# Stacking the left-over rows two groups earlier in a spectral filter kernel, with three more trips through memory

## The chip, the cores and the metric

The kernel runs on one core of a Trainium2 chip. The metric is the time of one execution in device microseconds; the time given for a kernel is the median of its runs.

## The reference

```python
h  = x + irfft2(rfft2(layernorm(x)) * (w_r + 1j * w_i))     # x: 2048 x 640, w: 2048 x 321
g, u = layernorm(h) @ w_gate, layernorm(h) @ w_up           # 640 x 1728 each
out = h + (g * u) @ w_down                                  # 1728 x 640
```

All of it is float32. The change lies in the first line, in the part that transforms along the 640 features.

## The kernel before, in words

The two-dimensional transform is done with matrix products. A first stage transforms along the 2048 rows in steps of 128 points. It leaves, for 16 groups `g`, the values of the 640 features folded by symmetry: four blocks of 128 features (`s1`, one for each kind of symmetry) and 128 left-over features, 31 to 33 of each kind (`rest`).

The **feature stage** then goes over the 16 groups. It is a software pipeline whose order is written out by hand: each engine runs its instructions in the order of the code, and a loop turn `g` holds work of four groups.

- `d_mm(g + 2)`, on TensorE (PE): the transform along the features into two banks `re` and `im`. The four main blocks are four float32 products of 160 to 193 columns each (`tab,s`).
- The left-over features are computed in a cheaper single-pass format, `fp32r`. For accuracy each value is split into a high and a low part: `rest_high` (ACT) and `rest_low` (DVE) write `s1r[:, 0]` and `s1r[:, 1]`. The product is then high x high + high x low + low x high.
- In a *plain* group this takes six products over all 128 left-over features and all 322 columns (`frt,s1r`). In a *stacked* group the 33 rows of one kind are laid under each other three times (high, low, high: 99 rows), and each kind needs one product of 160 to 194 columns, four in all (`frt,st`). `ST` holds the stacked groups; `PLAIN` says where they begin.
- To lay rows under each other, data must change partitions, so it goes through DRAM: `spread(a, b)` writes the split rows of groups a to b - 1 to `sfar` (four DMAs, one for each kind), and `stack(g, n, ...)` reads groups g to g + n - 1 back (two DMAs, of 66 and 33 rows). A read is issued only when the writes that it reads have landed.
- `d_out` (ACT) copies `re` and `im` to `t`; `s2_mm(g)` (PE) multiplies by a table (`bits`) into `u`, which from group 1 on has a single buffer; `filt(g)` (DVE, three instructions that read `u`) applies the weights `wts`; `add` (DVE) sums; `is2_mm(g - 1)` (PE, into `ir` and `im`) starts the way back, and `is2_parts` (ACT, DVE, POOL) takes it out to `qr` and `qm`.

The reads are placed by the table `AGAIN`: the key is the loop turn, the value the first group, the number of groups and the place. Before, groups 5 to 7 are read in turn 0 (place `dC`), 8 and 9 in turn 1 (`qt`), 10 to 12 in turn 4 and 13 to 15 in turn 7 (into the two halves of `s1r`, whose first contents are done with by then).

All these DMAs are issued by SyncE (SP), in one order: the tables `bits` (`load_mm`), the weights `wts` (`load_w`), writes and reads. A DMA issue that must wait holds up all that stand behind it. Eight DMAs of this queue can be under way: each waits for the one that was issued eight before it.

Of the kernel before, what the change touches and what calls it, by code (L numbers as in the profile page):

```python
# [12 lines left out]
F32R = mybir.dt.float32r  # L13
# [3 lines left out]
P = 128  # L17
S, D, NF, FF = 2048, 640, 321, 1728
NT = S // P
NG = 16  # L20
# [4 lines left out]
RROWS = ((31, 1), (0, 1), (62, 2), (63, 2))  # L25
RWHERE = ((1, 0), (0, 0), (1, 160), (0, 160))
RW = (160, 194, 162, 162)
PLAIN, MID = 5, 10
IPLAIN, IFAR = 5, 9
SUMS = 7  # L30
IPARTS = ((5, 4), (9, 3), (12, 4))
AGAIN = {0: (5, 3, "dC"), 1: (8, 2, "qt"), 4: (10, 3, 0), 7: (13, 3, 1)}
NR = 4
AHEAD = 5
FOLDS = {0: (1, 2), 1: (3,), 2: (4,), 7: (9,), 9: (11,)}
# [14 lines left out]
def f32(ap):  # L50
    return ap.bitcast(F32)
# [29 lines left out]
def tile_spectral_glu(ctx: ExitStack, tc: tile.TileContext, x, wre, wim, wgu, wlast, wdown, wdlast,  # L81
                      cc, ci, fmain, frem, imain, irem, mm, out):
    nc = tc.nc
# [52 lines left out]
    def home(tag, shape, name, dt=F32):  # L136
        return keep.tile(shape, dt, tag=tag, name=name)

    def cut(t, o, *shape):
        v = t[:, o:o + int(np.prod(shape))]  # L140
        names = [f"d{i}" for i in range(len(shape))]
        return v.rearrange(f"p ({' '.join(names)}) -> p {' '.join(names)}", **dict(zip(names[1:], shape[1:])))
# [6 lines left out]
    s1r = home("wA", [P, 2, NG, P], "s1r", F32R)  # L149
# [142 lines left out]
    def s1_rest(t):  # L292
        act(at(rest, t), PS1[t][1][:, 0:P].rearrange("p (g m) -> p g m", g=32), AF.Copy)
# [5 lines left out]
    def rest_high(a, b):  # L299
        act(s1r[:, 0, a:b], rest[:, a:b], AF.Copy)  # L300

    def rest_low(a, b):
        tt(s1r[:, 1, a:b], rest[:, a:b], f32(s1r[:, 0, a:b]), op=OP.subtract)
# [33 lines left out]
    for t in range(NT):  # L337
# [52 lines left out]
        else:  # L390
            b2a, b2, b3a, a2, b3, a3, m, v = stats[0]
# [6 lines left out]
        s1_mm(t)  # L398
    s1_main(NT - 1, PS1[NT - 1][0], 2, 4)
    s1_rest(NT - 1)  # L400
    for a, b in ((0, 2), (2, PLAIN), (PLAIN, MID)):
        rest_high(a, b)
        rest_low(a, b)

# [2 lines left out]
    def load_w(g):  # L407
        w, j = wts[:, g % 3], g // 2 if g < NG - 2 else g - 7
        i = wts[:, 5 if j == 8 else 3 + j % 2]
        nc.sync.dma_start(w, wre[g])  # L410
        if g % 2 == 0 or g >= NG - 2:
            nc.sync.dma_start(i, wim[j])
        W2[g] = w, i

    def load_mm(g, way):
        if g < NG:
            nc.sync.dma_start(mms[g % 4][:, way], mm[g][:, way])
# [10 lines left out]
    def d_mm(g):  # L428
        ps = PD[g] = bank("re"), bank("im")
        where = ((1, 0), (0, 0), (1, 160), (0, 160))  # L430
        main = [(b, o, FW[c], s1[:, c, g], fmt[:, FOFF[c]:FOFF[c] + FW[c]]) for c, (b, o) in enumerate(where)]
        if g not in ST:
            parts(ps, main, [(b, s1r[:, k, g], frt[:, l, b]) for k, l in ((0, 0), (0, 1), (1, 0)) for b in range(2)])
            return
        parts(ps, main, [])
        for q, ((b, o), w) in enumerate(zip(RWHERE, RW)):
            a = 4 * NQ + sum(RW[:q])
            mmx(ps[b][:, o:o + w], ST[g][0:99, q], frall[0:99, a:a + w], False, q >= 2)

    ST = {}  # L440
    sfar = far.tile([4, 2, 33, NG - PLAIN, P], F32, name="sfar")

    def spread(a, b):
        for q, (r, s) in enumerate(RROWS):
            nc.sync.dma_start(sfar[q, :, :, a - PLAIN:b - PLAIN].rearrange("l r g n -> r l g n"),
                              f32(s1r[r:r + 32 * s + 1:s, :, a:b]))

    def stack(g, n, tag):
        if tag in (0, 1):
            o = s1r[:, tag, NG - 12:NG].rearrange("p (q n) m -> p q n m", q=4)  # L450
        else:
            o = home(tag, [P, 4, n, P], "st", F32R)
        src = sfar[:, :, :, g - PLAIN:g - PLAIN + n].rearrange("q l r g n -> q (l r) (g n)")
        for a, b, r in ((0, 66, 0), (66, 99, 0)):
            nc.sync.dma_start(f32(o[a:b].rearrange("p q g n -> p q (g n)")),
                              src[:, r:r + b - a].rearrange("q r n -> r q n"))
        for i in range(n):
            ST[g + i] = o[:, :, i]

    def d_out(g, parts=(0, 1)):  # L460
        for i in parts:
            if i == 0:
                T[g] = wk([P, 2, NQ], "t")
            for h in range(2):
                act(T[g][64 * i:64 * i + 64, h], PD[g][i][64 * h:64 * h + 64, 0:NQ], AF.Copy)

    def s2_mm(g):
        if g >= NG - 2:
            ps = PU[g] = bank("re"), bank("im")
        elif g == 0:  # L470
            ps = PU[g] = bank("im2", 1), bank("ir2", 1)
        else:
            PU[g] = pools["y"].tile([P, 2, 512], F32, tag="u", name="u", bufs=1)
            ps = PU[g][:, 0], PU[g][:, 1]
        for h in range(2):
            nc.tensor.matmul(ps[h][:, 0:NQ], mms[g % 4][:, 0, h], T[g][:, h], start=True, stop=True)  # L476
# [18 lines left out]
    def filt_half(g, h, alone=False, mid=()):  # L495
        if h == 0:
            Y[g] = wk([P, 2, NQ], "y"), wk([P, 2, NQ], "us")
        y, us = (a[:, h] for a in Y[g])
        v, w, im = PU[g][h][:, 0:NQ], *W2[g]
        direct = lambda: tt(y, v, w[:, h], op=OP.mult)  # L500
        join = lambda: tt(y, y, us, op=OP.add)
        if alone:
            direct()
            for f in mid:
                f()
            nc.vector.scalar_tensor_tensor(us[0:64], v[64:128], -1.0, im[64:128, h], op0=OP.mult, op1=OP.mult)
            tt(us[64:128], v[0:64], im[0:64, h], op=OP.mult)
            return direct, join
        act(us[0:64], v[64:128], AF.Copy, scale=-1.0)
        act(us[64:128], v[0:64], AF.Copy)  # L510
        nc.gpsimd.tensor_tensor(us, us, im[:, h], op=OP.mult)
        return direct, join
# [52 lines left out]
    def is2_out(g):  # L565
        high, end, low, main, edges = is2_parts(g)
        high(copy)
        end(copy)
        low()
        main(slice(0, 4))  # L570
        edges(nc.gpsimd)

    for g in range(4):
        for way in range(2):
            load_mm(g, way)
        if g < 3:
            load_w(g)
    spread(PLAIN, MID)
    d_mm(0)
    d_out(0)  # L580
    d_mm(1)
# [1 line left out]
    for g in range(NG - 1):  # L583
        s2_mm(g)
        load_mm(g + 4, 0)
        if g + 2 < NG:
            d_mm(g + 2)
        if g + 3 == NG:
            xt = home("big", [P, 2, 5, 2, 512], "xt", F32R)
            flat = xt[:, 1].rearrange("p k l n -> p (k l n)")  # L590
            irt, sirt = cut(flat, 0, 5, NQ), cut(flat, 5 * NQ, 4, 162)
            scrap, near = cut(flat, 2258, D), cut(flat, 2258 + D, 4, 4, P)
        if g == NG - 2:
            nc.gpsimd.dma_start(flat[:, 0:2258], irem)
        if g == NG - 2:
            s2_mm(g + 1)
            filt_half(g, 0, True, (lambda: is2_out(g - 2),))
        if g >= 1:
            is2_mm(g - 1)
            load_mm(g + 3, 1)  # L600
        if g < NG - 2:
            add = filt(g)
        else:
            direct, _ = filt_half(g, 1)
            direct()
            late = [filt_half(g + 1, 0), filt_half(g + 1, 1, True)]
            high, end, low, main, edges = is2_parts(g - 1)
            late[0][0]()
            high(copy)
            end(copy)  # L610
            late[0][1]()
            late[1][1]()
            low()
            main(slice(0, 4))
            edges(nc.gpsimd)
        if g + 3 < NG:
            load_w(g + 3)
        if g >= 4 and g in AGAIN:
            stack(*AGAIN[g])
        if g == 0:  # L620
            rest_high(MID, NG)
        elif g == 1:
            rest_low(MID, NG)
            qr = home("qr", [P, 2, NT, P], "qr", F32R)
        if g + 2 < NG:
            d_out(g + 2, (0,))
            if 1 <= g < NG - 3:
                high, end, low, main, edges = is2_parts(g - 1)
                high(copy)
                end(copy)  # L630
            d_out(g + 2, (1,))
            add()
            if 1 <= g < NG - 3:
                low()
                main(slice(0, 4))
                edges(nc.gpsimd)
        if g < 2:
            stack(*AGAIN[g])
        elif g == 2:
            spread(MID, NG)  # L640
        if g == 9:
            nc.sync.dma_start(cit, ci)
            nc.sync.dma_start(imt, imain)
# [252 lines left out]
    for ts in (range(3), range(3, 6), range(6, 8)):  # L896
        n, t0 = len(ts), ts[-1] + 1
# [664 lines left out]
```

## Time and profile before

| | |
|---|---|
| median of 3 runs | 671.57 us (671.43 to 671.62) |
| profiled execution | 671.61 us, of which the profiled span is 669.8 us |
| busy: PE, DVE, POOL, ACT | 99%, 70%, 59%, 48% of the span |
| feature stage, `d_mm(0)` to the last `is2_mm` | 38.3 us to 106.0 us |

Times within the profile count from the start of the span. Busy times of PE overlap, since matrix products are pipelined, so a stretch of PE is measured here from the start of one instruction to the start of another. "SPq" rows are DMA issues: their duration is that of the issue, not of the transfer. In rows of stretches the columns are: stretch, length, busy time (and instructions) of PE, of its weight loads PEld, of DVE, ACT and POOL, then the granted TensorE clock, the mean busy share of the 16 DMA engines, and GB/s.

### The profile page before, as it was taken

Reading aid. Unit: us, or ns where it says so; the run is one execution under the profiler, and the core shown is the slowest. Engines: PE = TensorE matmul, PEld = TensorE weight load, DVE = VectorE, ACT = ScalarE, POOL = GpSimd, SP = SyncE. Lnnn points to the kernel's source line nnn. Section 1 sums busy time; section 2 is a strip of 40 time slices with the busy share of each in tenths; the row PEclk is TensorE's granted clock in tenths of the full one; section 3 lists DMA queues with packets and bytes.
Section 4 is the critical chain, followed back from the end, with each engine's and each line's share of the span. In section 5 each row is a group of like instructions: output and inputs, shape, how many; then the busy total and the mean of one; then the engine's idle time right before and its main releaser. Section 6 shows DMA issues by size and latency. Waiting matters only on the chain.

```text
span 669.8 us, 10242 instructions
## 1 busy us (share of the span) xinstructions
PE 660.0 (99%) x3695; PEld 587.1 (88%) x3695; DVE 468.7 (70%) x951; ACT 321.6 (48%) x621; POOL 394.5 (59%) x379
## 2 busy tenths in 40 slices
PE   6999999999999999999999999999999999999997
PEld 6999999887888888888888899888888888888887
DVE  6969997788767767594857567754757475757644
ACT  6977773585525243453626146634434251624220
POOL 3101124750397977969686445198786869697610
PEclk9999999999999999999999999999999999999999
DMA  8639885502212120042332467212011121212004
GB/s 320 226 109 282 237 252 160 160 1 79 79 40 80 39 79 28 34 99 59 99 78 84 93 134 260 78 41 74 13 37 76 41 78 40 79 40 80 1 0 158
DMA packets 48953, 66.12 MB, mean 99 GB/s; under 512 B 24082, under 2 KB 30670, under 8 KB 48774
## 3 DMA queue, kind: packets, MB, share of 16 engines
q1 hardware_dynamic: 48246, 62.91, 30.5%
q0 software_dynamic: 288, 2.16, 0.8%
q8 instruction: 29, 0.48, 0.3%
q10 hardware_dynamic: 368, 0.39, 0.2%
q14 instruction: 22, 0.18, 0.1%
HBM read 54.61 MB, written 10.84 MB: 98 GB/s over the span
## 4 chain that ended last, share of the span: by engine, by line
PE 95%; ACT 2%; DVE 1%; DMA 1%; issue 0%; POOL 0%; DVEq 0%
PE e L121 50%; PE d L121 26%; PE eo L121 4%; PE y L121 2%; PE re L121 2%; PE u L476 2%; PE im L527 2%; PE im L121 2%; PE im L270 2%; PE ir L527 1%; DMA x<-in_x_dram 1%; ACT s L296 1%; ACT fold L212 0%; ACT fold L211 0%; PE y L803 0%; PE u L527 0%
## 5 line engine op out<-in xcount | busy, mean ns | idle before, releaser
L121 PE MATMUL e<-xt,wst 128*128 128x512 f32 x864 | 211.1, 390 | 0.0
L121 PEld LDWEIGHTS e<-xt,wst 128*128 128x128 f32 x864 | 160.6, 188 | 31.7
L1082 DVE TENSOR_TENSOR x<-d,x 128x320 f32<-128x320 f32 x280 | 120.5, 483 | 41.2 <-PE d L121 37.0
L121 PE MATMUL d<-wd,ht 128*128 128x320 f32 x832 | 142.2, 309 | 0.0
L121 PEld LDWEIGHTS d<-wd,ht 128*128 128x128 f32 x832 | 129.6, 188 | 5.2
L996 POOL TENSOR_TENSOR wst<-raw,wst 128x1024 fp32r<-128x1024 f32 x23 | 55.5, 2412 | 69.5 <-ACT wst L995 69.5
L121 PE MATMUL e<-t,wst 128*128 128x512 f32 x360 | 94.0, 391 | 0.0
L121 PEld LDWEIGHTS e<-t,wst 128*128 128x128 f32 x360 | 66.7, 188 | 13.0
L121 PE MATMUL d<-wt,ht 128*128 128x320 f32 x360 | 69.0, 309 | 0.0
L1012 POOL TENSOR_TENSOR wst<-raw,wst 128x896 fp32r<-128x896 f32 (+1 forms) x46 | 65.3, 1444 | 0.2 <-ACT wst L1007 0.2
L121 PEld LDWEIGHTS d<-wt,ht 128*128 128x128 f32 x360 | 57.3, 188 | 0.8
L1098 ACT ACTIVATE ht<-e 128x512 fp32r<-128x512 f32 x44 | 26.4, 599 | 49.2 <-DVE e L1160 23.7
L1007 ACT ACTIVATE wst<-raw 128x896 fp32r<-128x896 f32 (+1 forms) x48 | 30.1, 676 | 31.2 <-POOL raw L1001 30.5
L1156 DVE TENSOR_TENSOR e<-e,h 128x512 f32<-128x512 f32 x24 | 16.8, 699 | 39.3 <-ACT wst L1007 23.1
L1057 DVE TENSOR_TENSOR x<-d,x 128x320 f32<-128x320 f32 x62 | 27.5, 485 | 22.4 <-PE d L121 22.3
L688 ACT ACTIVATE wd<-draw 128x320 fp32r<-128x320 f32 (+1 forms) x30 | 15.7, 560 | 55.1 <-POOL draw L698 52.4
L121 PE MATMUL e<-xt,wdir 128*128 128x512 f32 x180 | 42.1, 392 | 0.0
L1136 ACT ACTIVATE h<-e 128x512 f32<-128x512 f32 x24 | 14.3, 596 | 56.8 <-PE e L121 56.8
L121 PEld LDWEIGHTS e<-xt,wdir 128*128 128x128 f32 x180 | 33.4, 188 | 7.7 <-ACT xt L813 0.5
L1101 DVE TENSOR_TENSOR ht<-e,ht 128x512 fp32r<-128x512 f32 x54 | 37.0, 686 | 1.6 <-ACT ht L1098 1.3
L1153 ACT ACTIVATE h<-e 128x512 f32<-128x512 f32 x24 | 14.3, 598 | 46.7 <-PE e L121 46.7
L667 POOL TENSOR_TENSOR wd<-draw,wd 128x640 fp32r<-128x640 f32 x8 | 12.4, 1576 | 40.8 <-ACT wd L666 40.8
(239 smaller groups left out, 1188.1 us busy)
## 6 DMA issues: line engine op xcount, KB each, us to landing
raw<-in_wgu_dram SPq DMA_DIRECT2D x24, 640.0 KB
draw<-in_wdown_dram SPq DMA_DIRECT2D x24, 320.0 KB
wts<-in_wre_dram SPq DMA_DIRECT2D x16, 322.0 KB
x<-in_x_dram SPq DMA_DIRECT2D x15, 320.5 KB
out_dram<-x SPq DMA_DIRECT2D x15, 320.0 KB
bits<-in_mm_dram SPq DMA_DIRECT2D x32, 128.0 KB
wts<-in_wim_dram SPq DMA_DIRECT2D x9, 322.0 KB
zfar<-zr SPq DMA_DIRECT2D x32, 80.0 KB
```

The lines of the kernel that those rows point to most:

```text
L121: nc.tensor.matmul(o, l, r, start=start, stop=stop, skip_group_check=True)
L527: nc.tensor.matmul(out, y[:, h, a:b], inv(g, h), start=n == 0, stop=n == len(ys) - 1)
L688: act(o[:, 0, a:a + n], src, AF.Copy)
L996: ptt(wa[:, 1], stage[:, 0:1024], f32(wa[:, 0]), op=OP.subtract)
L1007: act(ws[:, 0, o:o + b - a], stage[:, a:b], AF.Copy)
L1012: ptt(ws[:, 1, o:o + b - a], stage[:, a:b], f32(ws[:, 0, o:o + b - a]), op=OP.subtract)
L1057: tt(xv, ps[b][:, 0:320], xv, op=OP.add)
L1082: tt(xv, o, xv, op=OP.add)
L1098: act(hop[:, a, 0], src, AF.Copy)
L1101: engine.tensor_tensor(hop[:, a, 1], src, f32(hop[:, a, 0]), op=OP.subtract)
L1136: act(h0, oa, AF.Copy)
L1156: tt(ob, ob, h1, op=OP.add)
```

## The change

Groups 3 and 4 become stacked groups (`PLAIN` from 5 to 3). Their rows must be written and read back before the loop begins, so the first write is cut in two: groups 3 to 5 first, then 6 to 9 (`NEXT`). Between the two stand two reads: group 3 alone, and groups 4 and 5 behind it. Both go into the place `dC`, which holds three groups. Groups 6 and 7 are read in turn 1, followed by group 8, which goes to the part of `dC` that group 3 has left; groups 9 to 11 in turn 4, 12 to 14 in turn 6, and 15 in turn 9, into the same part of `dC`. The splits are cut to match, and groups 3 to 5 are split ahead of group 2.

```diff
-PLAIN, MID = 5, 10
+PLAIN, NEXT, MID = 3, 6, 10
...
-AGAIN = {0: (5, 3, "dC"), 1: (8, 2, "qt"), 4: (10, 3, 0), 7: (13, 3, 1)}
+FIRST = ((3, 1, "dC", 0), (4, 2, "dC", 1))
+AGAIN = {1: ((6, 2, "qt", 0), (8, 1, "dC", 0)), 4: ((9, 3, 0, 0),), 6: ((12, 3, 1, 0),), 9: ((15, 1, "dC", 0),)}
...
-    for a, b in ((0, 2), (2, PLAIN), (PLAIN, MID)):
+    for a, b in ((0, 2), (PLAIN, NEXT), (2, PLAIN), (NEXT, MID)):
         rest_high(a, b)
         rest_low(a, b)
...
-    def stack(g, n, tag):
-        if tag in (0, 1):
-            o = s1r[:, tag, NG - 12:NG].rearrange("p (q n) m -> p q n m", q=4)
-        else:
-            o = home(tag, [P, 4, n, P], "st", F32R)
+    SH = {}
+
+    def stack(g, n, tag, at):
+        if tag not in SH:
+            SH[tag] = s1r[:, tag, NG - 12:NG].rearrange("p (q n) m -> p q n m", q=4) if tag in (0, 1) else home(
+                tag, [P, 4, 3 if tag == "dC" else n, P], "st", F32R)
+        o = SH[tag][:, :, at:at + n]
...
-    spread(PLAIN, MID)
+    spread(PLAIN, NEXT)
+    for job in FIRST:
+        stack(*job)
+    spread(NEXT, MID)
     d_mm(0)
```

The other lines of the diff only walk through the new form of the table.

On PE, from `s2_mm(1)` to `s2_mm(2)` (L476 `u<-t`), the products of group 3 read as follows before. `tab,s` are the main products, `frt,s1r` the left-over ones, `ir` and `im` of L527 the way back of group 0.

```order
L121 MATMUL im<-tab,s_89 128x160
L121 MATMUL re<-tab,s_89 128x193
L121 MATMUL im<-tab,s_89 128x161
L121 MATMUL re<-tab,s_89 128x161
L121 MATMUL re<-frt,s1r 128x322
L121 MATMUL im<-frt,s1r 128x322
...
L527 MATMUL ir_647<-bits,y 65x32x4 x2
L527 MATMUL im_646<-bits,y 128x32x4 x4
L476 MATMUL u<-t,bits 128x322 x2
```

Four more left-over products of 322 columns stand in the gap. The same place now (line numbers are one or two higher):

```order
L122 MATMUL im<-tab,s_89 128x160
L122 MATMUL re<-tab,s_89 128x193
L122 MATMUL im<-tab,s_89 128x161
L122 MATMUL re<-tab,s_89 128x161
L122 MATMUL im<-frt,st 128x160
L122 MATMUL re<-frt,st 128x194
L122 MATMUL im<-frt,st 128x162
L122 MATMUL re<-frt,st 128x162
L529 MATMUL ir_653<-bits,y 65x32x4 x2
L529 MATMUL im_652<-bits,y 128x32x4 x4
L478 MATMUL u<-t,bits 128x322 x2
```

Group 3 has four left-over products instead of six, and they read `st`, which a DMA fills; group 4 one turn later likewise.

On SP, from the first write on, the order before is this (`sfar<-s1r` is a write, `st<-sfar` a read of 66 or 33 rows; 128 columns are one group):

```order
L445 DMA sfar<-s1r 33x2x640 x4
L417 DMA bits<-in_mm_dram 128x256
L410 DMA wts<-in_wre_dram 128x644
L455 DMA st<-sfar 66x4x384
L455 DMA st<-sfar 33x4x384
L417 DMA bits<-in_mm_dram 128x256 x2
L410 DMA wts<-in_wre_dram 128x644
L412 DMA wts<-in_wim_dram 128x644
L455 DMA st<-sfar 66x4x256
L455 DMA st<-sfar 33x4x256
```

And now, up to the first load behind the second write:

```order
L446 DMA sfar<-s1r 33x2x384 x4
L458 DMA st<-sfar 66x4x128
L458 DMA st<-sfar 33x4x128
L458 DMA st<-sfar 66x4x256
L458 DMA st<-sfar 33x4x256
L446 DMA sfar<-s1r 33x2x512 x4
L418 DMA bits<-in_mm_dram 128x256
L411 DMA wts<-in_wre_dram 128x644
```

Four reads and four writes have moved ahead of the table of group 4 and the weights of group 3, and the first of these reads stands right behind the write that it reads.

More of the change, by code (lines that the diff above doesn't have):

```diff
@@ L446, in spread @@
                               f32(s1r[r:r + 32 * s + 1:s, :, a:b]))
-    def stack(g, n, tag):
-        if tag in (0, 1):
-            o = s1r[:, tag, NG - 12:NG].rearrange("p (q n) m -> p q n m", q=4)
-        else:
-            o = home(tag, [P, 4, n, P], "st", F32R)
[L453 to L456, printed above, removed]
+    SH = {}
[4 more added lines that the diff above has]
+        o = SH[tag][:, :, at:at + n]
+        src = sfar[:, :, :, g - PLAIN:g - PLAIN + n].rearrange("q l r g n -> (l r) q (g n)")
+        for a, b in ((0, 66), (66, 99)):
+            nc.sync.dma_start(f32(o[a:b].rearrange("p q g n -> p q (g n)")), src[0:b - a])
         for i in range(n):
@@ L617, in tile_spectral_glu @@
             load_w(g + 3)
-        if g >= 4 and g in AGAIN:
-            stack(*AGAIN[g])
+        if g >= 4:
+            for job in AGAIN.get(g, ()):
+                stack(*job)
         if g == 0:
@@ L636, in tile_spectral_glu @@
                 edges(nc.gpsimd)
-        if g < 2:
-            stack(*AGAIN[g])
-        elif g == 2:
+        if g < 4:
+            for job in AGAIN.get(g, ()):
+                stack(*job)
+        if g == 2:
             spread(MID, NG)
```

## The prediction

> **What bounds the kernel now.** I read the page's busy shares and its chain first, then the timeline of PE over the group loop, then DVE and the DMA queue over the same microseconds.
>
> ```profile
> PE 660.0 (99%) x3695; PEld 587.1 (88%) x3695; DVE 468.7 (70%) x951; ACT 321.6 (48%) x621; POOL 394.5 (59%) x379
> PE 95%; ACT 2%; DVE 1%; DMA 1%; issue 0%; POOL 0%; DVEq 0%
> ```
>
> PE is busy for 99% of the span and is 95% of the chain that ended last. What PE is spared in the group loop shortens the run, unless another engine takes the place over at once. So the question is how near the next engine is. The PE timeline from the left-over products of group 3 to those of group 5 (columns: start us, us, what):
>
> ```profile
> 47.70 0.42 PE L121 MATMUL re<-frt,s1r 128*128 128x322 f32 x1
> ...
> 48.70 0.60 PE L527 MATMUL ir<-bits,y 128*65 128x128 f32 x4
> ...
> 50.03 1.25 PE L476 MATMUL u<-t,bits 128*128 128x322 f32 x4
> ...
> 52.16 0.42 PE L121 MATMUL re<-frt,s1r 128*128 128x322 f32 x1
> ...
> 53.16 0.60 PE L527 MATMUL ir<-bits,y 128*65 128x128 f32 x4
> ...
> 54.48 1.25 PE L476 MATMUL u<-t,bits 128*128 128x322 f32 x4
> ...
> 56.61 0.35 PE L121 MATMUL im<-frt,st 99*128 99x160 f32 x1
> ...
> 57.13 0.60 PE L527 MATMUL ir<-bits,y 128*65 128x128 f32 x4
> ...
> 58.47 1.26 PE L476 MATMUL u<-t,bits 128*128 128x322 f32 x4
> ```
>
> Groups 3 and 4 spend 48.70 - 47.70 = 53.16 - 52.16 = 1.00 us on six left-over products of 322 columns. Group 5 is stacked and spends 57.13 - 56.61 = 0.52 us on four. One loop turn is 54.48 - 50.03 = 4.45 us with a plain group and 58.47 - 54.48 = 3.99 us with a stacked one. The same stretch on DVE:
>
> ```profile
> 46.86 0.83 DVE L484 TENSOR_TENSOR y<-u,wts 128x644 f32<-128x644 f32 x1 [0.61 <-PE u L476]
> ...
> 49.42 0.96 DVE L303 TENSOR_TENSOR s1r<-rest,s1r 128x768 fp32r<-128x768 f32 x1
> ...
> 51.61 0.83 DVE L484 TENSOR_TENSOR y<-u,wts 128x644 f32<-128x644 f32 x1
> ...
> 53.32 0.82 DVE L486 TENSOR_TENSOR us<-u,wts 64x644 f32<-64x644 f32 x1
> ...
> 55.77 0.83 DVE L484 TENSOR_TENSOR y<-u,wts 128x644 f32<-128x644 f32 x1 [0.32 <-PE u L476]
> ...
> 57.48 0.82 DVE L486 TENSOR_TENSOR us<-u,wts 64x644 f32<-64x644 f32 x1
> ```
>
> Here the reader sees a second clock. From 46.86 to 51.61 DVE has no gap: the filter of group 1, the split of groups 10 to 15 (0.96 us at 49.42, in this turn alone) and the sums. The filter of group 2 thus begins at 51.61 because DVE is free only then, and it holds `u`, which has one buffer, until 53.32 + 0.82 = 54.14. PE refills `u` at 54.48, only 0.34 us later. In a stacked turn DVE holds it to 57.48 + 0.82 = 58.30, and PE comes at 58.47.
>
> **The change part by part.** *Two groups fewer with six products.* PE is spared 2 x (1.00 - 0.52) = 0.96 us. If all of it counted, the run would take 671.61 - 0.96 = 670.65 us.
>
> *What `u` leaves of it.* Nothing ahead of group 3's products changes on PE, so DVE still starts at 46.86 and still reaches the filter of group 2 at 51.61, and `u` still comes free at 54.14. PE would arrive there at 54.48 - 0.96 = 53.52. It waits, and with some 0.06 us for the hand-over (55.77 against the end of the products at 54.48 + 1.25 = 55.73 shows 0.04) it starts at 54.20. The gain that is left is 54.48 - 54.20 = 0.28 us, and 0.68 us turn into a wait of PE for DVE. One turn later DVE starts at 54.20 + 1.25 + 0.04 = 55.49 and frees `u` at 58.02, while PE comes at 54.20 + 3.99 = 58.19: no second wait, and the 0.28 us stay. This also gives group 3 slack: its products may end 0.68 us later than they could before they cost anything.
>
> *The write and the read that group 3 now needs.* Rows of the DMA queue (SPq, columns as above), of the wait on it, and the two splits on DVE that release the first write:
>
> ```profile
> 39.76 0.56 DVE L303 TENSOR_TENSOR s1r<-rest,s1r 128x384 fp32r<-128x384 f32 x1
> 40.39 0.83 DVE L303 TENSOR_TENSOR s1r<-rest,s1r 128x640 fp32r<-128x640 f32 x1
> 41.25 2.54 SPq L445 DMA_DIRECT2D sfar<-s1r  x4
> 43.89 0.45 SPq L417 DMA_DIRECT2D bits<-in_mm_dram  x1
> 45.26 0.35 SPq L410 DMA_DIRECT2D wts<-in_wre_dram  x1
> 46.63 0.75 SPq L455 DMA_DIRECT2D st<-sfar  x2
> SPq L455 <- DMA sfar<-s1r: 0.9, 1, 0.9
> ```
>
> Stretches of the DMA engines (the last two columns are their busy share and GB/s):
>
> ```profile
> 41.25:42.00 0.75, 0.75 (x7) 0.75 (x6) 0.00 (x0) 0.70 (x3) 0.00 (x0) 1.00 0.00 0
> 42.00:46.00 4.00, 4.00 (x25) 3.59 (x24) 2.70 (x6) 3.23 (x7) 0.00 (x0) 1.00 0.64 196
> 44.00:52.00 8.00, 8.00 (x53) 7.34 (x53) 7.15 (x12) 5.24 (x12) 1.83 (x2) 1.00 0.72 190
> 52.00:72.00 20.00, 20.00 (x142) 18.36 (x141) 18.54 (x26) 15.08 (x37) 3.68 (x10) 1.00 0.95 281
> ...
> 121.00:122.00 1.00, 1.00 (x9) 1.00 (x9) 0.96 (x3) 0.27 (x1) 1.00 (x2) 1.00 0.08 32
> 122.00:125.50 3.50, 3.50 (x23) 3.07 (x22) 3.43 (x9) 2.51 (x5) 3.28 (x3) 1.00 0.68 179
> 125.50:127.00 1.50, 1.50 (x10) 1.29 (x9) 1.12 (x2) 1.50 (x5) 1.46 (x2) 1.00 0.00 0
> 128.50:134.00 5.50, 5.50 (x35) 4.79 (x34) 4.18 (x14) 2.15 (x6) 3.09 (x5) 1.00 0.60 147
> ```
>
> The write of five groups went out at 41.25, when DVE's split of 640 columns had ended (40.39 + 0.83). The new first write needs only the 384 columns in second place, done at 39.76 + 0.56 = 40.32, so it goes out at 40.35. Before, 0.75 us passed with nothing moving, then 4 us of traffic (0.8 us a group), then 0.6 us until the queue was let go at 46.63. Three groups are 0.75 + 2.4 + 0.6 = 3.75 us: done at 44.1. Then group 3 is read. The trace shows a read by itself in the next stage, where three groups of the same shape are issued at the row below and move from 122.0 to 125.5, 1.2 us a group:
>
> ```profile
> 121.06 0.32 SPq L727 DMA_DIRECT2D si<-ifar  x1
> ```
>
> One group is 0.95 + 1.2 + 0.6 = 2.75 us, so its rows are there at 46.85, and PE wants them at 47.70. Bounds: no moving time at all gives 45.65; a moving time set by the number of pieces, which is the same for one group as for three, gives 44.1 + 0.95 + 3.5 + 0.6 = 49.15. I take 46.85, since bytes set it in the two reads that the trace shows alone: three groups are 0.68 x 3.5 = 2.38 us of the engines, four groups in as many pieces (128.5 to 134) are 0.60 x 5.5 = 3.30, a ratio of 1.39 against 1.33 by bytes. With the slack of 0.68 us group 3 may come as late as 48.4.
>
> *Groups 4 and 5 behind it* move 2.4 us more and are there at 46.85 + 2.4 = 49.25. Group 4's products begin at 52.16 - 0.48 = 51.68.
>
> *What is pushed back on the queue.* Eight further issues, the four reads and the second write, now stand ahead of the loads of 43.89 and 45.26. At some 0.4 us each (0.75 for two at 46.63) and 2.54 for the write, the weights of group 3 leave at about 44.1 + 1.6 + 2.5 + 0.5 = 48.7. The DMA engines are behind with older traffic then, so they wait for 3.6 us of reads and 4 x 0.8 = 3.2 us of writes that run from 45.05 to 51.9, and land by some 53.5. Their reader is the filter that started at 55.77, now 55.49. This costs nothing as long as the DMA engines keep up.
>
> *One more piece of the split* (128 + 512 instead of 640 columns) is one more instruction on ACT and on DVE. By the two DVE rows (0.56 us for 384, 0.83 for 640) one costs 0.15 us besides its columns, and DVE idles 0.61 us ahead of 46.86 as cover; ACT's piece is of that size too. *Group 8's read* waits for group 3's products to be done with their place, long past when it is issued. Reads of 9 to 15 move between groups; one of these matters and is the first rival.
>
> Sum: 671.61 - 0.96 + 0.68 = 671.33 us for the profiled execution (span 669.8); against the median of 671.57 that is 671.29. I say 671.3.
>
> **The rivals.** *Group 9 waits for its read: slower.* What was the read of groups 10 to 12 becomes that of 9 to 11, at the same place in the loop and wanted one turn earlier.
>
> ```profile
> 63.49 1.14 SPq L455 DMA_DIRECT2D s1r<-sfar  x2
> ...
> 71.72 0.33 SPq L417 DMA_DIRECT2D bits<-in_mm_dram  x1
> ...
> SPq L417 <- DMA s1r<-sfar: 0.2, 1, 0.2
> ...
> 72.56 0.35 PE L121 MATMUL im<-frt,st 99*128 99x160 f32 x1
> ```
>
> The load at 71.72 had waited for this read, so it took 71.7 - 63.49 = 8.2 us. Group 9's products stand at 72.56, so 72.56 - 63.49 = 9.07 us are there: 0.87 to spare. Ahead of it the DMA engines now have one group more to read (1.2 us) and two more to write (1.6 us), 2.8 in all. From 52 to 72 us they are 95% busy and can't catch up. They can start 0.9 earlier, and the stretch from 44 to 52 is only 72% busy, which holds (0.95 - 0.72) x 8 = 1.8 us. Used fully, 0.1 us is left and the read is in time. If only the early start helps, it is 1.9 late, PE waits 1.9 - 0.87 = 1.0 us, and the run takes 671.33 + 1.0 = 672.35. It decides from 0.87 + 0.28 = 1.15 us of backlog on: then the run is slower than before. Chance 0.26.
>
> The Trainium skill (DMA: Bandwidth & Descriptors, Bandwidth) speaks against the change here: its table has 0.95 us for 64 KB and 6.15 us for 1 MB, so small transfers pay a floor of roughly 0.6 us, an estimate from these two. Two reads more ahead of group 9's would by it add 1.2 us to the 0.1 above, PE would wait 0.4 us, and the run would take some 671.8 us. The rows of before can't separate a floor from the idle 0.95 us ahead of a read, so I leave its weight within this rival.
>
> *Group 3 is late.* If pieces and not bytes set the read, it lands at 49.15, PE idles 49.15 - 47.70 = 1.45 us, 0.48 + 0.48 of it is paid back by shorter products, and `u` is refilled at 54.48 + 1.45 - 0.96 + 0.05 = 55.02: 671.61 + 0.54 = 672.15. Against it speaks the ratio of 1.39 above. Later still, the price grows one for one: a read of 8.2 us, the slowest that a row of before shows (the fence above), would end at 52.3. The Trainium skill (TensorE: Matmul & The Clock Gate, The HAM clock gate) has the clock halved after an idle window of some 3.4 us, which only such a wait of 4.6 us would reach. The stretches above show the granted clock at 1.00 throughout. Chance 0.09.
>
> *The full saving.* If PE did not meet the held `u`, 670.65. The gapless DVE rows from 46.86 to 54.14 speak against it. Chance 0.06.
>
> *Nothing gained*: DVE's chain starts later than the timeline says (its 46.86 start follows PE's `u` of group 1, and ACT and DVE have one more split ahead), by the 0.28 us that are left. 671.6, chance 0.07.
>
> **How the numbers follow.** The forecast keeps 0.52. The range reaches down to 670.9, short of the full saving, and up to 672.9, over most of the late reads; outside lie the full saving (0.06), a third of the group 9 cases and a third of the late group 3 (0.12 together): 0.18. A change under 0.2%, 1.34 us, is about what a measurement of this kernel can't tell from none; no case is faster by that much, 0.02 for what I don't see. Slower by it needs over 672.9, 0.12. The rest, 0.86, is the same. The forecast's own range is 671.0 to 671.6.
>
> **What would show it.** Right: groups 3 and 4 with four left-over products of 0.52 us; a wait of PE of 0.5 to 0.7 us at its `u` refill near 54.2 that is put down to DVE; the first write at 40.35, group 3's read issued near 44.1 and no wait of PE at its products; the end of the group loop about 0.3 us earlier. Wrong: PE waiting for a DMA at the products of group 3 or group 9, DVE waiting for weights, or the loop's end later than before while the stages behind it are unchanged.

## The result and the profile after

The changed kernel takes 676.49 us in the median of seven runs (673.17 to 677.63), beside 671.62 us for the kernel before on the same chip: a ratio of 1.0061 with a 95% interval of 1.0051 to 1.0071. It is slower by some 5 us where 671.3 was forecast. Its runs scatter over 4.5 us; the profiled execution is one of its shorter ones, with 673.93 us and a span of 672.2.

The busy shares and the chain:

```profile
PE 661.6 (98%) x3691; PEld 587.5 (87%) x3691; DVE 468.7 (70%) x952; ACT 321.3 (48%) x622; POOL 394.0 (59%) x379
PE 88%; DMA 4%; ACT 3%; DVE 2%; POOL 1%; issue 1%; SPq 0%; DVEq 0%; ACTq 0%
```

DMAs have grown from 1% to 4% of the chain. The waits of PE in the feature stage that are new (columns: us in total, times, longest):

```profile
PE im L122 <- DMA s1r<-sfar: 1.3, 1, 1.3
PE u L478 <- DVE us L488: 0.4, 1, 0.4
```

The PE timeline shows where:

```profile
47.71 0.35 PE L122 MATMUL im<-frt,st 99*128 99x160 f32 x1
48.23 0.60 PE L529 MATMUL ir<-bits,y 128*65 128x128 f32 x4
...
54.29 1.32 PE L478 MATMUL u<-t,bits 128*128 128x322 f32 x4 [0.42 <-DVE us L488]
...
58.34 1.26 PE L478 MATMUL u<-t,bits 128*128 128x322 f32 x4
...
74.04 0.31 PE L122 MATMUL im<-frt,s1r 99*128 99x160 f32 x1 [1.33 <-DMA s1r<-sfar]
```

Group 3's left-over products start at 47.71 with no wait and take 48.23 - 47.71 = 0.52 us. PE waits for DVE at `u` (54.29). At 58.34 it is 0.13 us ahead of the kernel before. At 74.04 it has waited 1.33 us for the read of groups 9 to 11, and is 74.04 - 72.56 = 1.48 us behind. The stage ends 1.4 us later (107.4 against 106.0). The other 0.9 us of the longer span lie in later stages that the change doesn't touch; I don't explain them. In the profiled executions of the other kernels below these stages take at most 0.7 us longer than before, and where a kernel loses more than 1 us, most of it lies in the feature stage.

SP's queue, in the changed kernel:

```profile
40.36 2.54 SPq L446 DMA_DIRECT2D sfar<-s1r  x4
44.75 1.60 SPq L458 DMA_DIRECT2D st<-sfar  x4
46.39 2.44 SPq L446 DMA_DIRECT2D sfar<-s1r  x4
48.93 0.46 SPq L418 DMA_DIRECT2D bits<-in_mm_dram  x1
...
57.30 3.71 SPq L446 DMA_DIRECT2D sfar<-s1r  x4
...
64.89 0.82 SPq L458 DMA_DIRECT2D s1r<-sfar  x2
...
73.92 0.76 SPq L458 DMA_DIRECT2D s1r<-sfar  x2
```

the row of the third write (groups 10 to 15) in the kernel before:

```profile
55.60 2.65 SPq L445 DMA_DIRECT2D sfar<-s1r  x4
```

and the waits of SP in the changed kernel that bear on it:

```profile
SPq L458 <- DMA sfar<-s1r: 1.7, 1, 1.7
SPq L446 <- DMA wts<-in_wim_dram: 1.0, 1, 1.0
SPq L446 <- DMA st<-sfar: 1.4, 2, 0.8
SPq L458 <- DMA s1r<-sfar: 1.0, 1, 1.0
```

The third write goes out 1.7 us later and its four issues take 1.1 us longer. The first of them waits 1.0 us for the weights that were issued eight places ahead of it, the next two 1.4 us for the read of groups 6 and 7. The read of groups 9 to 11 stands behind this write on SP and needs it landed. It is issued at 64.89, 1.40 us later than the read at the same place before. The profile names no wait of SP between the write and this issue, so as far as the rows show it is the queue's order that makes the read late, and not a wait for the landing. SP's next read waited for this one, so it took until 73.9: 9.0 us from its issue, where it was 8.2. The stretches of the DMA engines (last two columns: busy share and GB/s):

```profile
44.00:48.00 4.00, 4.00 (x26) 3.67 (x26) 3.27 (x7) 2.88 (x6) 1.55 (x1) 1.00 0.32 65
44.00:52.00 8.00, 8.00 (x53) 7.26 (x53) 7.15 (x12) 5.23 (x12) 1.83 (x2) 1.00 0.56 165
```

From 44 to 52 us they carry less than before (0.56 against 0.72), although more was to be moved: SP waits 1.7 us for the first write to land ahead of the read at 44.75, and the table of group 4 and the weights of group 3 leave only from 48.93 on.

### The profile page after: what moved, and what is told of

Same layout as the page of the kernel before. It is cut to its first block, busy times and chain, and to the rows that moved or that the text cites. A ratio compares the mean times of both kernels' runs of the same rounds, so it can differ in the third digit from the quotient of the medians.

```text
span 672.2 us, 10254 instructions
## 1 busy us (share of the span) xinstructions
PE 661.6 (98%) x3691; PEld 587.5 (87%) x3691; DVE 468.7 (70%) x952; ACT 321.3 (48%) x622; POOL 394.0 (59%) x379
## 4 chain that ended last, share of the span: by engine, by line
PE 88%; DMA 4%; ACT 3%; DVE 2%; POOL 1%; issue 1%; SPq 0%; DVEq 0%; ACTq 0%
PE e L122 48%; PE d L122 24%; PE eo L122 4%; PE y L122 2%; PE u L478 2%; PE re L122 2%; PE im L529 2%; PE im L271 2%; PE im L122 1%; DMA s1r<-sfar 1%; DMA z<-zfar 1%; DMA raw<-in_wgu_dram 1%; PE ir L529 1%; DMA x<-in_x_dram 1%; ACT s L297 1%
```

## The experiments

**Is the wait for group 9 the whole loss?** The changed kernel once more:

> The changed kernel once more, to see how its executions spread. In the profile of it PE waits 1.3 us for the read of groups 9 to 11 and the run is 673.9 us, yet four of seven executions took 676.5 to 677.6 us at a mean granted clock of 0.996 to 0.997 instead of 1.000. Theory (late read): these have a longer wait at the same place, 2 to 3 us, and a stretch of lowered clock behind it: again 673 to 678 us, never under 672.5. Rival (something else lowers the clock, the wait is a bystander): the long executions show the same 1.3 us wait and lose their time in another stage.

676.5 us (674.26 to 678.38), ratio 1.007 (1.0054 to 1.0086). The profiled execution has other waits of PE than the first one:

```profile
PE im L122 <- DMA s1r<-sfar: 2.4, 1, 2.4
...
PE u L478 <- issue: 1.2, 1, 1.2
...
PE im L122 <- DMA st<-sfar: 0.5, 1, 0.5
```

Group 6's read (`st`) is late too, and at one `u`, at 72.63, PE waits 1.2 us with no releaser named ("issue"). DVE's rows tell why: its filter had waited 1.53 us for weights, and so it held the one buffer `u` until then.

```profile
70.00 0.83 DVE L486 TENSOR_TENSOR y<-u,wts 128x644 f32<-128x644 f32 x1 [1.53 <-DMA wts<-in_wre_dram]
```

These waits are 4.1 us together, and the stage ends at 110.9, 4.9 us later than before. So in an execution of about the median time (676.87) nearly the whole loss lies in this stage. Then I gave group 9 a read of its own, one turn earlier:

```diff
-AGAIN = {1: ((6, 2, "qt", 0), (8, 1, "dC", 0)), 4: ((9, 3, 0, 0),), 6: ((12, 3, 1, 0),), 9: ((15, 1, "dC", 0),)}
+AGAIN = {1: ((6, 2, "qt", 0), (8, 1, "dC", 0)), 3: ((9, 1, "dC", 1),), 4: ((10, 3, 0, 0),), 7: ((13, 3, 1, 0),)}
```

> The changed kernel with group 9 read alone in turn 3 into the place that group 4 has left, and groups 10 to 12 and 13 to 15 in turns 4 and 7 as in the kernel before: as many reads, writes and bytes as the changed kernel, but nothing that is read in turn 4 is wanted before turn 8. Theory (late read): no wait of PE for a DMA in the feature stage, the clock stays at 1.000, and what is left is the gain cut by the single buffer of u: 671.3 to 671.4 us. Rival (the ten DMAs more overload the queue, whichever read comes last): another read or the weights come late instead, 672.5 us or more. Rival (the clock falls for another reason): executions of 675 to 678 us remain.

675.49 us, ratio 1.0054 (1.0042 to 1.0066). No wait for group 9, and the loss stays:

```profile
PE u L478 <- issue: 1.3, 1, 1.3
PE u L478 <- PE im L529: 0.5, 1, 0.5
...
DVE y L486 <- DMA wts<-in_wre_dram: 2.6, 2, 1.6
```

Both waits of PE at `u` stand behind a filter that waited for weights (0.9 us at 72.85 and 1.6 us at 78.32). The wait has moved to another load, as the first rival had it.

**The lead alone, and a late read alone.** In the kernel before, only the reads regrouped, so that the read of turn 4 begins with group 9 in place of 10:

```diff
-AGAIN = {0: (5, 3, "dC"), 1: (8, 2, "qt"), 4: (10, 3, 0), 7: (13, 3, 1)}
+AGAIN = {0: (5, 3, "dC"), 1: (8, 1, "qt"), 4: (9, 3, 0), 7: (12, 3, 1), 9: (15, 1, "dC")}
```

> The kernel before (groups 3 and 4 plain, one write of five groups) with the reads cut as in the changed kernel from group 8 on: 5 to 7, 8, 9 to 11 in turn 4, 12 to 14 in turn 7, 15 in turn 9. Group 9 is wanted one turn earlier, without the extra write and reads ahead of it. Theory (backlog from the added transfers makes it late): in time or late by under 0.3 us, 671.5 to 672.0 us. Rival (one turn less of lead is too short by itself): PE waits over 1 us for this read, 672.6 us or more, and executions with a lowered clock.

672.02 us, ratio 1.0005 (0.9997 to 1.0014), no wait of PE for a DMA. The shorter lead costs nothing that can be told as long as nothing else is added. For the price of one late read, the kernel before with the read of groups 10 to 12 two turns later:

```diff
-AGAIN = {0: (5, 3, "dC"), 1: (8, 2, "qt"), 4: (10, 3, 0), 7: (13, 3, 1)}
+AGAIN = {0: (5, 3, "dC"), 1: (8, 2, "qt"), 6: (10, 3, 0), 7: (13, 3, 1)}
```

> The kernel before with the read of groups 10 to 12 issued in turn 6 instead of 4, and nothing else: it then goes out at about 71.5 us and lands at 77.5 to 79.5, and PE wants it at 76.55. Theory (a wait of PE for a read costs its length, and a longer one also the clock): PE idles 1 to 3 us at the products of group 10 and the run takes 672.6 to 674.6 us, plus 2 to 3 us in executions where the clock falls. Rival (the clock falls for another reason): the wait costs its length alone, and the clock stays at 1.000 in all executions.

676.45 us, ratio 1.0068 (1.0053 to 1.0084). The profiled execution (676.07) has a single wait:

```profile
PE im L121 <- DMA s1r<-sfar: 2.8, 1, 2.8
```

That execution lost 4.4 us, more than the wait: the clock fell behind it, as told below. The one run of six with a mean clock of 1.000 took 673.59 us, the others, at 0.995 to 0.997, 675.8 to 677.8.

**Transfers or PE's earlier demand?** The changed kernel with all its transfers, but with groups 3 and 4 multiplied plain:

```diff
-        if g not in ST:
+        if g not in ST or g in (3, 4):
```

> The changed kernel with all its writes and reads, but groups 3 and 4 multiplied as plain groups with six left-over products (what was read for them is not used). PE is spared nothing. Theory (the added transfers alone make the loads of later groups late): PE waits 1 to 4 us for DMAs or tables from group 6 on, 673 to 677 us. Rival (PE's earlier demand matters, the transfers are hidden when PE comes as late as before): within 0.2% of before, 671.3 to 672.3 us.

674.97 us, ratio 1.0053 (1.0034 to 1.0072), and the same wait:

```profile
PE im L122 <- DMA s1r<-sfar: 1.3, 1, 1.3
```

The transfers do the harm without any help from a faster PE.

**Bytes or number?** The changed kernel less two loads of weights, and the kernel before plus ten tiny DMAs:

```diff
-        nc.sync.dma_start(w, wre[g])
+        if g not in (5, 6):
+            nc.sync.dma_start(w, wre[g])
```

> The changed kernel without the loads of wre for groups 5 and 6 (these groups are filtered with the weights that lie in their place; everything else is issued and computed as in the changed kernel). It takes away 2 x 322 KB just ahead of the late loads; the change added 2 x (132 + 198) = 660 KB. Theory (bytes: the DMA engines have more to move than fits before the loads are wanted): PE waits for a DMA for less than 0.4 us in all, no stretch of lowered clock, 671.4 to 671.9 us. Rival (the ten DMAs more in SP's one order, with eight under way at most, are what makes loads late): the waits stay, 673 us or more.

```diff
...
+    def tiny(a, b):
+        for i in range(a, b):
+            nc.sync.dma_start(speck[i:i + 1], f32(s1r[0:1, 0, 0]))
...
+    tiny(0, 6)
...
+        if g in (1, 9):
+            tiny(*((6, 8) if g == 1 else (8, 10)))
```

> The kernel before with ten more DMAs of one row of 512 bytes each on SP's queue, at the places where the changed kernel has ten more: six behind the first write, two ahead of the read of groups 8 and 9, two in turn 9. No other byte is moved. Theory (it is the bytes and pieces of the added groups that the DMA engines can't carry in time): no wait of PE for a DMA, 671.3 to 672.0 us. Rival (SP's queue: more DMAs under the limit of eight under way make SP late, whatever they move): the read of groups 10 to 12 lands after 72.5 or other loads are late, 672.5 us or more.

Without the weights 673.09 us, ratio 1.0026 (1.0016 to 1.0036): more than half of the loss is gone, not all. The theory had put this at 671.9 at most, and the median lies at the rival's 673; the edit also takes two DMAs out of the queue. The tiny DMAs cost nothing that can be told: 671.79 us, ratio 1.0005 (0.9996 to 1.0013), no wait for a DMA. So the number alone isn't it. But the number of bytes alone isn't either. The kernel before with as many bytes more, in two copies that nothing waits for:

```diff
...
         nc.sync.dma_start(w, wre[g])
+        if g in (5, 6):
+            nc.sync.dma_start(ballast[g - 5], wre[g])
```

> The kernel before with two more DMAs, each of which copies 322 KB of wre (groups 5 and 6) in DRAM to a place that nothing reads, right behind the loads of the same weights; 644 KB against the 660 KB that the change added. Everything else stands as before the change. Theory (the bytes are the cause): PE waits 1 us or more for a load wanted after 60 us, 672.6 us or more, some executions with a lowered clock. Rival (the new order and the early reads are needed for the harm): no wait of PE for a DMA, 671.4 to 672.1 us.

671.88 us, ratio 1.0009 (1.0000 to 1.0018), no wait for a DMA. My theory in its strong form is wrong. The queue shows why nothing waits:

```profile
65.39 0.81 SPq L459 DMA_DIRECT2D s1r<-sfar  x2
...
73.76 1.09 SPq L421 DMA_DIRECT2D bits<-in_mm_dram  x2
```

```profile
SPq L421 <- DMA s1r<-sfar: 1.0, 1, 1.0
```

The load at 73.76 had to wait for the read, which was issued at 65.39, 1.9 us later than before: it lands 2.0 us later than before (71.72), as late as in the changed kernel. But here it brings groups 10 to 12, and 10 is wanted a turn of 3.99 us after group 9's 72.56. Had it brought group 9, PE would have waited some 73.7 - 72.56 = 1.1 us. So neither the lead alone (0.87 us to spare is left) nor the load alone (some 2.8 us to spare) makes a wait, and by these rows the two together would; a kernel with just these two was not tried.

**Order.** The changed kernel with the table and the weights that had been pushed back put where they were:

```diff
-    for job in FIRST:
-        stack(*job)
-    spread(NEXT, MID)
     d_mm(0)
...
         load_mm(g + 4, 0)
+        if g == 0:
+            stack(*FIRST[0])
...
             load_w(g + 3)
+        if g == 0:
+            stack(*FIRST[1])
+            spread(NEXT, MID)
```

> The changed kernel with the table of group 4 issued ahead of group 3's read and the weights of group 3 right behind it; the read of groups 4 and 5 and the second write come behind them. Same transfers, another order. In the changed kernel the DMA engines were 0.32 busy from 44 to 48 us, before the change 0.67: 1.4 us of their work was put off. Theory in two parts (2.8 us of added work and 1.4 us put off by the order): the order alone brings back part, PE's waits for DMAs shrink from 1.3 to 4 us to 0.3 to 1.5 us, 671.8 to 673.5 us; group 3's products wait at most 0.6 us. Rival (added bytes alone): no difference from the changed kernel, 675 to 677 us. Rival (order alone): no wait for a DMA, 671.3 to 671.6 us.

675.93 us, ratio 1.0066 (1.0054 to 1.0078): no gain, as its first rival had it, though the engines are busy again from 44 to 48 us, 0.60 against 0.32.

```profile
44.00:48.00 4.00, 4.00 (x27) 3.67 (x26) 3.27 (x7) 3.02 (x7) 1.50 (x1) 1.00 0.60 134
```

PE's waits:

```profile
PE im L122 <- DMA s1r<-sfar: 1.8, 1, 1.8
PE im L122 <- DMA st<-sfar: 0.8, 1, 0.8
```

Group 4 is now late as well, and group 9 as before. Then the third write one turn earlier:

```diff
-        if g == 2:
+        if g == 1:
             spread(MID, NG)
```

> The changed kernel with the write of groups 10 to 15 one turn earlier, right behind the reads of groups 6 to 8. Same transfers. In the changed kernel this write was issued at 57.3 us (before the change 55.6) and the read of groups 9 to 11, which needs it landed, 1.4 us later than before. Theory A (that chain alone makes group 9 late, and the rest keeps up): the read is issued near 63.4 us, PE waits less than 0.4 us for it and for no other load, 671.4 to 671.9 us. Theory B (the DMA engines have too much to move, and what is brought forward puts something else back): a load of another place is late, PE waits 1 us or more in all, 673 us or more.

673.44 us, ratio 1.0026 (1.0018 to 1.0034), and no lowered clock in twelve runs: more than half of the loss is gone, which the new order ahead of the loop had not brought about. The profiled execution is the shortest of the twelve (672.05), so it can't show all of the 1.9 us that the median still loses. In it group 9's read is in time; what is late is a load of weights, by which DVE frees `u` later:

```profile
DVE y L486 <- DMA wts<-in_wre_dram: 0.9, 1, 0.9
...
PE u L478 <- PE im L529: 0.5, 1, 0.5
```

Both orders together, with all of `FIRST` behind the table (`load_mm(g + 4, 0)` of turn 0), the weights of group 3 ahead of the second write, and group 8's read one turn later:

```diff
-AGAIN = {1: ((6, 2, "qt", 0), (8, 1, "dC", 0)), 4: ((9, 3, 0, 0),), 6: ((12, 3, 1, 0),), 9: ((15, 1, "dC", 0),)}
+AGAIN = {1: ((6, 2, "qt", 0),), 2: ((8, 1, "dC", 0),), 4: ((9, 3, 0, 0),), 6: ((12, 3, 1, 0),), 9: ((15, 1, "dC", 0),)}
...
             load_w(g + 3)
+        if g == 0:
+            spread(NEXT, MID)
...
```

> The changed kernel with its transfers in a better order: the table of group 4 ahead of group 3's read, the weights of group 3 ahead of the second write, the write of groups 10 to 15 right behind the read of groups 6 and 7, and group 8's read one turn later, behind it. Same bytes, same DMAs. Theory (work put off before the loop, plus the chain from the third write to the read of groups 9 to 11, plus bytes): PE waits for DMAs for at most 0.6 us in all, 671.3 to 672.2 us. Rival (bytes alone, any order): a load of another place is late, as with the earlier write alone, 673 us or more.

674.38 us, ratio 1.0042 (1.0028 to 1.0056): by the median 2 us less than the change, though the intervals of the two ratios touch, and no better than the early write alone. The wait at `u` is again one behind late weights:

```profile
PE u L478 <- issue: 1.3, 1, 1.3
PE im L122 <- DMA s1r<-sfar: 1.1, 1, 1.1
...
DVE y L486 <- DMA wts<-in_wre_dram: 1.6, 1, 1.6
```

The same without the two loads of weights:

> As order_both, and without the loads of wre for groups 5 and 6 (these groups are filtered with the weights that lie in their place), 644 KB less. Theory (bytes and order together are the whole loss): no wait of PE for a DMA, only that for DVE at u, no lowered clock, 671.2 to 671.6 us, the end of the feature stage 0.1 to 0.3 us earlier than before the change. Rival (a cause that was not found): 672.2 us or more.

672.31 us, ratio 1.0014 (1.0004 to 1.0023). The profiled execution, with a span of 670.2, has a single new wait of PE in the stage, that for DVE:

```profile
PE u L479 <- DVE us L489: 0.4, 1, 0.4
```

So taking away load and changing the order together bring back nearly all of the loss. About 0.7 us of the median stay unexplained, and with them the median lies just inside the range of the rival, a cause that was not found (672.2 or more). That other executions had a late load which the profiled one, at 671.94, had not is likely, not shown.

**Fewer groups, other queues, other pieces.** In the kernel before, group 4 alone stacked in addition:

```diff
-PLAIN, MID = 5, 10
+PLAIN, MID = 4, 10
...
-AGAIN = {0: (5, 3, "dC"), 1: (8, 2, "qt"), 4: (10, 3, 0), 7: (13, 3, 1)}
+AGAIN = {0: (4, 3, "dC"), 1: (7, 2, "qt"), 4: (9, 3, 0), 7: (12, 3, 1), 9: (15, 1, "dC")}
```

> The kernel before with group 4 alone as one more stacked group: groups 4 to 6 read in turn 0, 7 and 8 in turn 1, 9 to 11 in turn 4, 12 to 14 in turn 7, 15 in turn 9. Half of the added bytes (330 KB), one read (two DMAs) more, nothing cut in pieces ahead of the loop. Theory (bytes and pieces): half of the backlog; PE waits 0 to 1 us for DMAs, 671.3 to 672.6 us, and the wait of PE for DVE at the u near 54.3 stays. Rival (the cut first write and its early reads did the harm): no wait for a DMA, 671.2 to 671.5 us.

673.1 us, ratio 1.0025 (1.0016 to 1.0033), above the theory's range. Half of the load still costs 1.5 us, at another place: group 4 waits for the read of turn 0.

```profile
PE im L121 <- DMA st<-sfar: 0.9, 1, 0.9
```

In the changed kernel, all reads issued by GpSimd (`nc.gpsimd.dma_start` in `stack`), and then only those from group 6 on:

```diff
-            nc.sync.dma_start(f32(o[a:b].rearrange("p q g n -> p q (g n)")), src[0:b - a])
+            (nc.sync if g < 6 else nc.gpsimd).dma_start(f32(o[a:b].rearrange("p q g n -> p q (g n)")), src[0:b - a])
```

> The changed kernel with its seven reads issued by GpSimd on its own DMA queue; the writes, tables and weights stay on SP's. Theory B (DMA engines overloaded): loads are late all the same, PE waits 1 us or more, 673 us or more. Rival (SP's order and its limit of eight under way hold the loads up): SP's loads go out in time, PE waits less than 0.4 us for DMAs, 671.2 to 672 us. A read issued by GpSimd may take another time than on SP's queue; that would show at group 3.

> The changed kernel with the reads from group 6 on issued by GpSimd on its own DMA queue; groups 3 to 5 are read on SP's queue as in the changed kernel. In the run with all reads on GpSimd PE waited 4.5 us for group 3 and for no DMA later. Theory (the reads do their harm by standing in SP's one queue, ahead of tables and weights and behind them): no wait of PE for a DMA from group 6 on, only the 0.4 us for DVE at u stays, 671.2 to 671.7 us. Rival (that run had no later waits only because its loop began 7 us late, with the loads ahead of it): PE waits 1 us or more from group 6 on, 673 us or more.

All reads on GpSimd: 679.55 us, ratio 1.0114 (1.0101 to 1.0127), with one wait of 4.5 us for group 3 and a mean clock of 0.994 to 0.997. The later ones alone: 675.28 us, ratio 1.006 (1.0047 to 1.0074), with late reads of two kinds and a wait at `u` for which the profile names no load:

```profile
PE u L478 <- issue: 1.3, 1, 1.3
PE im L122 <- DMA st<-sfar: 0.4, 1, 0.4
...
PE im L122 <- DMA s1r<-sfar: 0.4, 1, 0.4
```

That the reads do their harm by standing in SP's one queue is not borne out: off it, two of the reads are late all the same. It isn't a clean test, since the reads now stand in GpSimd's order; one half of group 8's read goes out at 61.14, after 5.46 us in which GpSimd does nothing else. Last the reads in pieces of 64 and 32 rows:

```diff
-        for a, b in ((0, 66), (66, 99)):
-            nc.sync.dma_start(f32(o[a:b].rearrange("p q g n -> p q (g n)")), src[0:b - a])
+        for a, b, r in ((0, 64, 0), (66, 98, 0), (64, 66, 64), (98, 99, 32)):
+            nc.sync.dma_start(f32(o[a:b].rearrange("p q g n -> p q (g n)")), src[r:r + b - a])
```

> The changed kernel with each read cut in other pieces: 64 rows and 32 rows, and the 2 rows and 1 row that are left over, in four DMAs in place of two of 66 and 33 rows. Same bytes, 14 DMAs more. Where reads of 66 and 33 rows run alone the 16 DMA engines are at most 0.68 busy, near 11/16 = 0.69 (66 and 33 divide by 11, not by 16), while the weights' loads of 128 rows are at 0.95 and more in a row. Theory (reads of 66 and 33 rows lie on 11 of 16 engines, so they and all behind them take longer): reads land 1 to 2 us sooner after their issue than in the changed kernel (8.5 to 9 us for that of groups 9 to 11), PE waits less than 0.6 us for DMAs in all, 671.3 to 672.3 us. Rival (the total of bytes is what counts): as the changed kernel, 673 us or more.

679.17 us, ratio 1.0116 (1.0102 to 1.0129), the worst of all without a lowered clock:

```profile
PE u L478 <- issue: 2.5, 2, 1.3
PE im L122 <- DMA st<-sfar: 1.9, 2, 1.5
PE im L122 <- DMA s1r<-sfar: 1.2, 1, 1.2
```

The Trainium skill (DMA: Bandwidth & Descriptors, Rules for kernel authors) asks for all 16 engines by a slowest dimension that is a multiple of 16. Here pieces of 64 and 32 rows, which obey it, came with the left-over rows in DMAs of their own, 14 DMAs more behind a backlog, and the kernel was 2.7 us slower than the change itself; no run parts the shape from the number. Ten tiny DMAs cost nothing in a kernel whose queue had room. In this program each DMA of SP holds one of eight places until it lands, so I take the number to count where landings are slow; no run varied it by itself there.

**The saving that DVE eats.** light_weights with the subtraction of groups 10 to 15 on GpSimd:

```diff
...
-            rest_low(MID, NG)
+            rest_low(MID, NG, nc.gpsimd)
```

> As light_weights (no loads of wre for groups 5 and 6), and the split of groups 10 to 15 (subtraction of 768 columns, 0.96 us on DVE at 49.4 us) is done on GpSimd. Theory (DVE's filter of group 2 holds the one buffer u, and that ate 0.7 to 0.8 of the 0.96 us saved): the wait of PE for DVE at its u near 54.3 is gone, the products of group 5 start 0.7 to 1.0 us earlier than in the kernel before, 670.6 to 671.0 us if the loads keep up. Rival (something else holds u, or GpSimd slows DVE by as much): the same wait, 671.3 to 671.9 us.

672.38 us, ratio 1.0008 (1.0000 to 1.0017). The wait for DVE is gone and the products into `u` stand earlier, here those at the place of 54.48:

```profile
53.78 1.29 PE L479 MATMUL u<-t,bits 128*128 128x322 f32 x4
```

Counted from the stage's first product (38.43 here, 38.34 before), 53.78 is 0.79 us earlier than 54.48 was. What takes it back is PE's wait for the read of groups 9 to 11:

```profile
PE im L122 <- DMA s1r<-sfar: 0.8, 1, 0.8
```

On top of the better order, with all weights loaded:

> As order_both, and the split of groups 10 to 15 (subtraction, 0.96 us on DVE) on GpSimd, so that DVE comes to the filter of group 2 earlier. Theory: no wait of PE for DVE at its u near 54.3, up to 0.96 us of the saving is kept ahead of the first late load; if at most 0.6 us of waits for DMAs are left, 670.6 to 671.4 us, the fastest of all. Rival (PE comes 0.7 us earlier everywhere and only waits longer for the same loads): the same time as order_both within 0.3 us.

674.92 us, ratio 1.0045 (1.0032 to 1.0058), as order_both: PE comes sooner and waits as long or longer. No version that was run beats the kernel before.

## Why the prediction was wrong, point by point

- *Two groups with four products in place of six:* right in kind, 0.52 us of products each. Mis-sized: with DVE out of the way two groups brought 0.79 us, not 0.96 (light_pool).
- *What `u` leaves of it:* the wait for DVE came at the place named, 0.42 us against 0.5 to 0.7. Of the 0.28 us that were to stay, 0.13 stayed. These two terms are off by tenths and don't matter for the result.
- *Group 3 in time:* right. The first write went out at 40.36, the read at 44.75 (forecast 44.1), and no products of groups 3 to 5 waited. Its price for a piece-bound read was not needed.
- *"This costs nothing as long as the DMA engines keep up":* the step that failed. The sum has no term for the added transfers, and the engines did not keep up: PE waited 1.33 us for the read of groups 9 to 11 in the one profiled execution of the change, and 4.1 us for that read, group 6's read and weights in the other; the kernel takes 4.9 us more. The same transfers with nothing spared on PE cost it 3.5 us (load_plain), so they are the cause by themselves.
- *The first rival* had the mechanism and the place, with a chance of 0.26, but its sum was wrong. It let 1.8 us of the added 2.8 be carried by the idle share from 44 to 52 us; that stretch carried less, not more (0.56 for 0.72, or 1.3 us put off), because the write and read ahead of the loads wait for landings. It kept the issue of group 9's read at 63.49; it went out 1.40 us later, because it stands on SP behind a third write that the added DMAs had made late, and it took 9.0 us in place of 8.2. That is 2.2 us later, of which 0.87 were to spare. And it priced a late read at 1.0 us at most; the profiled executions of the change show 1.33 and 2.4. The floor of 0.6 us for each small transfer, by which the prediction also reckoned, no run here shows: ten DMAs of 512 bytes cost nothing that can be told (tiny_ten).
- *One read was examined.* The sum asked whether group 9 is in time, and no other load. After the change most loads have little to spare, so what is mended at one place is lost at the next: group 6's rows, group 4's rows, weights (again_pool, tables_first, nine_alone). The shorter lead alone and the bytes alone made no wait (lead_only, before_heavy); that it takes both to make group 9 late is worked out from their rows. How the rest divides between bytes, pieces and places in the queue stays open.
- *The clock* was left out, as only a wait of 4.6 us was to reach it. It fell after waits of 1.8 and 2.8 us, and in most kernels the runs in which it fell are the slowest.

## What to carry to other kernels

Where the DMA engines are busy for nine tenths of a stage, an added round trip through DRAM is not priced at its transfer time against an average idle share. List every load of the stage with its slack, and follow the queue from write to read, since what stands behind a delay moves with it. When an engine's wait has no releaser named, look at the engine that holds the buffer: here DVE's waits for weights told what PE's did not. A saving of under 1 us on PE is not worth any risk of one PE wait near 2 us: that wait can cost as much again in clock.

## What the runs showed of the hardware that was not expected

*The clock after a wait.* In the profiled execution of light_weights PE waits 1.8 us for group 9 and starts again at 74.40. Then (the third column from the end is the granted clock):

```profile
75.00:76.00 1.00, 1.00 (x11) 1.00 (x10) 0.00 (x0) 0.84 (x2) 0.00 (x0) 0.94 0.80 272
76.00:77.00 1.00, 1.00 (x5) 0.88 (x5) 0.25 (x1) 0.93 (x4) 0.00 (x0) 0.50 0.73 207
77.00:78.00 1.00, 1.00 (x3) 0.68 (x2) 0.17 (x1) 0.96 (x3) 0.68 (x2) 0.50 0.86 184
78.00:79.00 1.00, 1.00 (x4) 0.65 (x3) 0.07 (x1) 0.24 (x1) 0.04 (x1) 0.50 1.02 257
79.00:80.00 1.00, 1.00 (x8) 1.00 (x7) 0.97 (x2) 0.00 (x0) 0.00 (x0) 0.86 1.11 215
```

The clock is halved for some 3.4 us, which loses 0.06 + 3 x 0.50 + 0.14 = 1.7 us; this begins near 75.9, 1.5 us after PE has work again. The waits of 2.8 us in late_ten and 1.8 us in tables_first did the same. It isn't certain: after_again's 2.4 us left the clock at 1.00. Of the twelve runs of light_weights the three with a mean clock of 0.997 took 675.1 to 675.3 us, the others 671.9 to 673.3. In write_early and reads_wide, whose profiled executions have no wait above 1.5 us, no run fell below 0.999. The Trainium skill (TensorE: Matmul & The Clock Gate, The HAM clock gate) has a free-running window of about 3.4 us. The length of the slow stretch agrees with that; that an idle time of 1.8 us suffices does not agree with its rule of a whole idle window, and here the measurement decides.

*Engine time isn't bytes.* Two stretches of the kernel before, the first with reads of 66 and 33 rows among the loads, the second with tables and weights:

```profile
66.00:71.50 5.50, 5.50 (x38) 4.87 (x37) 5.18 (x8) 4.41 (x12) 0.73 (x2) 1.00 1.00 239
84.00:87.50 3.50, 3.50 (x27) 3.17 (x26) 3.39 (x5) 2.52 (x7) 0.41 (x1) 1.00 1.04 350
```

Fully busy engines move 239 GB/s in the one and 350 / 1.04 = 337 in the other. So by this rate 644 KB of weights taken away are a smaller load than the 660 KB of the change, which fits what light_weights left. The copies of before_heavy run within DRAM, and no stretch shows their rate.
